# A recorded order table in place of a list scheduler, with four v buffers, six raw buffers and a split of batch 0's exponent inputs, in a fused linear-attention and gated-FFN kernel

## The chip, the cores and the metric

The kernel runs on one core of one Trainium2 chip. The metric is device microseconds of one execution. Five engines work side by side: PE (TensorE, matrix products), DVE (VectorE), ACT (ScalarE), POOL (GpSimd) and SP (SyncE), whose queue issues every DMA here.

## The reference

Linear attention over 8 batches, 8 heads, 576 positions and head dimension 64, then a feed-forward block of width 512 to 1024 and back, with a convolution of three taps and a sigmoid gate:

```
def phi(x):
    proj = np.einsum('bhsd,df->bhsf', x, w_phi)
    proj = proj - np.max(np.abs(proj), axis=-1, keepdims=True)
    return np.concatenate([np.exp(proj), np.exp(-proj)], axis=-1)
q_p, k_p = (phi(q), phi(k))
kv = np.einsum('bhsf,bhsd->bhfd', k_p, v)
z = np.sum(k_p, axis=2)
num = np.einsum('bhsf,bhfd->bhsd', q_p, kv)
den = np.einsum('bhsf,bhf->bhs', q_p, z)[..., None] + 1e-06
attn = num / den
...
h = np.maximum(x @ w_in, 0.0)            # x: attn, heads joined
conv_out = sum(conv_w[k] * hp[:, k:k + S, :] for k in range(3))
out = (h * (1 / (1 + np.exp(-conv_out)))) @ w_out
```

The feed-forward weights come in double precision and are rounded on the chip.

## The kernel before

**Attention.** A unit is one piece of one batch's q or k: `project` loads raw data (tiles rk, rq; tag raw), multiplies it with `w_phi` on PE (tiles pk, pq in PSUM), and takes the maximum of the absolute value along the features on DVE (mk, mq). For every q and for the k of batches 1 to 7, DVE then subtracts that maximum into an SBUF tile (sk, sq), and ACT makes the two exponentials of it (ke; for q after a transpose tp on PE, qe). For the k of batch 0 the subtraction is left out: ACT negates the maximum (the small `mk<-mk` instruction) and makes the exponential straight out of PSUM with the maximum as a bias, one instruction of 128 columns for each of the unit's column groups (`ke<-pk,mk`). The list `KBU` says for each of batch 0's five units and each of its two halves which of the two ways is taken: 'b' is the bias, any other letter the subtraction. A k unit then multiplies ke with v (`kv`, accumulated in PSUM, copied to kvf). A q unit multiplies qe with kvf (`nm`); the denominator dn (on ACT for the batches in `DNA`, else on DVE), its reciprocal rc and the product x follow.

In tile names the numbers after the letters are batch (where it is kept), head group, column piece h, and half: rk0_0_2_1 is batch 0, group 0, piece 2, second load.

**Feed-forward.** The 4608 positions are cut into 11 chunks. For each: xt (transposes of x), xh and xl (a high and a low part), hp (three products for each of 4 x 8 blocks), h, c (convolution), a sigmoid over the whole chunk (ACT has to load its table before it, and the exponential's table again afterwards), gh and gl, op, os and the store. hp and op need no exponentials and are the bulk of PE's work. The weights' rounding (w_r, w_t, win_hi, win_lo, cw) is spread over DVE, ACT and POOL in the first part of the run.

**What sets the order.** Every instruction group is first recorded with `plan.add` (engine, a cost in ns, what it reads and writes, a rank). `Plan.order` is a list scheduler: it keeps a clock for each engine from these costs, and picks at each step the engine that is free first and on it the ready work of the lowest rank. The ranks are shifted by a table of numbers, `NUDGE`. Buffers are given out in the same pass (`Plan.place`). The result is one static order for each engine; each engine then runs its own list and waits only for what its instructions need. SP's list is of this kind too: a DMA that waits for a free buffer holds up all DMAs behind it.

Of the kernel before, what the change touches and what calls it, by code (L numbers as in the profile page):

```python
# [7 lines left out]
F32 = mybir.dt.float32  # L8
# [3 lines left out]
AF = mybir.ActivationFunctionType  # L12
# [4 lines left out]
F = 128  # L17
DM, FF = 512, 1024
P = 128
# [16 lines left out]
LANDING = 1600  # L36
PSUM_G = 4
# [12 lines left out]
SLACK = 60.0  # L50
# [9 lines left out]
RAW = 5  # L60
QS = 2
QE = 3
V = 2
OS = 2
KVF = 6
KBU = ('bb', 'bb', 'bb', 'bb', 'bb')
DNA = (0, 1)
# [3 lines left out]
NUDGE = """  # L71
# [43 lines left out]
"""  # L115
EDGE = [64 * n for n in EDGES]
NCH = len(EDGE) - 1
HW = max(b - a for a, b in zip(EDGE, EDGE[1:]))
TC = max(HW, 450)


class Piece:


    def __init__(self, pool, shape, dtype, name, slots, psum=False):
# [18 lines left out]
class Plan:  # L144
# [90 lines left out]
    def order(self):  # L235
# [6 lines left out]
        if len(shift) == len(self.groups):  # L242
            for w in self.works:
                w.rank += shift[w.group]
# [65 lines left out]
def kernel(  # L310
# [252 lines left out]
    def q_unit(b, qd, h, r):  # L563
        n, ps, m, pr = project(qT, b, qd, h, "q", r)
        x = piece([P, n, 2, D], F32, f"x{b}_{qd}_{h}", "x0" if h == 0 else "x", 2 if h == 0 else NXX)
        for q in range(2):
            if h == 0 or q == qd:
                xs[b, q, h] = x
# [276 lines left out]
```

## Time and profile before

| | |
|---|---|
| median of 3 runs | 708.52 us (708.51, 708.52, 711.76) |
| the profiled execution, its own time | 710.4 us |
| its span, first to last instruction | 708.4 us |
| mean granted PE clock | 0.995 |
| PE busy | 693.5 us, 98% |
| DVE, ACT, POOL busy | 478.5, 430.9, 72.6 us |

The span is the time between the first and the last instruction; what the execution takes beside it is not in the trace. Busy is the time in which at least one instruction of the engine ran. The end of a matmul is modelled, so that a busy PE need not be at its peak. PEclk, where a view shows it, is the clock that PE was granted, as a share of full speed.

### The profile page before, as it was taken

What the parts mean: (1) busy time and instruction counts of PE and PEld (TensorE: products, weight loads), DVE (VectorE), ACT (ScalarE), POOL (GpSimd) and SP (SyncE); (2) the same over time, 40 slices, a digit from 0 to 9 for tenths busy, and PEclk for the clock granted to TensorE, in tenths of its full rate; (3) what the DMA queues carried; (4) which work ended last, traced back from release to release, by engine and by line L of the source; (5) the groups of instructions that cost most, each with busy time, mean ns of one, the idle gap of its engine ahead of it and who ended that gap; (6) DMA issues with size and microseconds to landing.
All of it is one profiled execution on the core that took longest, in us unless ns stands there. A gap on an engine that the chain in (4) does not pass through costs nothing. (4 is left out here: it accounts for less than half of the span.)

```text
span 708.4 us, 22055 instructions
## 1 busy us (share of the span) xinstructions
PE 693.5 (98%) x9484; PEld 639.3 (90%) x9484; DVE 478.5 (68%) x1030; ACT 430.9 (61%) x821; POOL 72.6 (10%) x103
## 2 busy tenths in 40 slices
PE   6998999999999999999999999999999999999998
PEld 5886899899999999999999989999998899999997
DVE  4797998989796286776538675788259544567350
ACT  7977788785774465674349365755567343655351
POOL 0343213350010010000001000100100000101000
PEclk9999999999999999999999999999999999999999
DMA  7563543341212022222202311112002110000001
GB/s 211 163 203 112 153 116 101 103 110 50 69 58 61 22 71 79 73 70 66 64 13 76 106 42 46 57 33 61 27 27 70 35 40 15 14 24 13 36 27 52
DMA packets 46609, 49.00 MB, mean 69 GB/s; under 512 B 6320, under 2 KB 44464, under 8 KB 46512
## 3 DMA queue, kind: packets, MB, share of 16 engines
q1 hardware_dynamic: 46512, 47.59, 22.6%
q8 instruction: 75, 1.23, 0.7%
q14 instruction: 22, 0.18, 0.1%
HBM read 38.13 MB, written 9.44 MB: 67 GB/s over the span
## 5 line engine op out<-in xcount | busy, mean ns | idle before, releaser
L698 DVE SCALAR_TENSOR_TENSOR c<-h,cw,c 128x254 f32<-128x254 f32 (+11 forms) x256 | 122.7, 520 | 100.0 <-ACT c L688 98.7
L675 PE MATMUL hp<-xh,win_hi 128*128 128x448 f32 (+2 forms) x352 | 128.7, 366 | 0.8 <-ACT h L685 0.7
L739 PE MATMUL op<-gh,wout_hi 128*128 128x448 f32 (+3 forms) x352 | 127.6, 362 | 0.0
L739 PE MATMUL op<-gl,wout_hi 128*128 128x448 f32 (+3 forms) x352 | 124.7, 354 | 0.1
L739 PE MATMUL op<-gh,wout_lo 128*128 128x448 f32 (+3 forms) x352 | 124.3, 353 | 0.0
L675 PE MATMUL hp<-xh,win_lo 128*128 128x448 f32 (+2 forms) x352 | 123.9, 352 | 0.0
L675 PE MATMUL hp<-xl,win_hi 128*128 128x448 f32 (+2 forms) x352 | 123.8, 352 | 0.0
L582 ACT ACTIVATE qe<-tp 128x512 f32<-128x512 f32 (+1 forms) x160 | 79.8, 566 | 46.3 <-PE tp L578 46.0
L518 ACT ACTIVATE ke<-sk 128x512 f32<-128x512 f32 (+1 forms) x140 | 74.2, 595 | 41.2 <-DVE sk L492 22.0
L685 ACT ACTIVATE h<-hp 128x448 f32<-128x448 f32 (+2 forms) x88 | 45.5, 518 | 65.0 <-PE hp L675 63.7
L593 PE MATMUL nm<-kvf,qe 128*64 128x65 f32 x2304 | 78.9, 224 | 0.3 <-ACT qe L582 0.2
L682 POOL COPY h<-h 128x3 f32<-128x3 f32 x64 | 28.0, 437 | 478.3 <-DVE c L707 262.5
L593 PEld LDWEIGHTS nm<-kvf,qe 128*64 128x64 f32 x2304 | 73.3, 139 | 3.9 <-issue 2.7
L549 PE MATMUL kv<-v,ke 128*64 128x65 f32 x2048 | 72.5, 226 | 4.5 <-DMA v<-in_vt_dram 3.0
L549 PEld LDWEIGHTS kv<-v,ke 128*64 128x64 f32 x2048 | 66.5, 140 | 8.7 <-ACT w_t L391 3.3
L675 PEld LDWEIGHTS hp<-xh,win_hi 128*128 128x128 f32 x352 | 66.1, 188 | 7.1 <-issue 1.5
L739 PEld LDWEIGHTS op<-gh,wout_hi 128*128 128x128 f32 x352 | 66.2, 188 | 4.7 <-issue 1.2
L739 PEld LDWEIGHTS op<-gl,wout_hi 128*128 128x128 f32 x352 | 66.3, 188 | 4.0 <-DVE gl L719 0.3
L739 PEld LDWEIGHTS op<-gh,wout_lo 128*128 128x128 f32 x352 | 66.4, 189 | 3.3
L675 PEld LDWEIGHTS hp<-xl,win_hi 128*128 128x128 f32 x352 | 66.0, 188 | 3.5
L675 PEld LDWEIGHTS hp<-xh,win_lo 128*128 128x128 f32 x352 | 66.2, 188 | 3.1
L719 DVE TENSOR_TENSOR gl<-c,gh 128x896 fp32r<-128x896 f32 (+3 forms) x44 | 43.5, 1025 | 34.1 <-ACT gh L716 34.0
(58 smaller groups left out, 965.2 us busy)
## 6 DMA issues: line engine op xcount, KB each, us to landing
v<-in_vt_dram SPq DMA_DIRECT2D x80, 130.0 KB, 2.5
rk<-in_kT_dram SPq DMA_DIRECT2D x64, 128.0 KB, 2.6
rq<-in_qT_dram SPq DMA_DIRECT2D x64, 128.0 KB, 2.3
w_r<-in_w_in_dram SPq DMA_DIRECT2D x8, 512.0 KB, 4.1
w_r<-in_w_out_dram SPq DMA_DIRECT2D x8, 512.0 KB, 3.7
out_dram<-os SPq DMA_DIRECT2D x12, 191.0 KB, 2.0
out_dram<-os SPq DMA_DIRECT2D x12, 161.0 KB, 1.8
out_dram<-os SPq DMA_DIRECT2D x8, 225.0 KB, 2.3
```

Source lines behind the costliest of these rows:

```text
L518: act(*((627, 520) if n == 4 else (417, 306)), lambda s=s, e=e, j=j: nc.scalar.activation(out=e[s](), in_=pr[j](), func=AF.Exp, scale=1.0 ...
L549: nc.tensor.matmul(out=kp()[a : a + 64, s, t // 2 * VW : (t // 2 + 1) * VW], lhsT=es[j][s]()[:, t, a : a + 64], rhs=vs[t // 2]()[:, c : c ...
L582: act(*((597, 478) if n == 4 else (384, 264)), lambda s=s, tp=tp, qe=qe: nc.scalar.activation(out=qe()[:, s], in_=tp(), func=AF.Exp, scale ...
L593: nc.tensor.matmul(out=ps_()[a : a + 64, t, :], lhsT=qe()[:, s, t, a : a + 64], rhs=kv[b, q][j]()[:, s, p0 * VW : (p0 + 1) * VW], start=(s ...
L675: nc.tensor.matmul(out=ps()[:, :W], lhsT=w, rhs=x, start=(p == 0 and k == 0), stop=(p == 3 and k == 2))
L682: pool(405, 375, lambda hs=hs, old=old: nc.gpsimd.tensor_copy(out=hs()[:, :3], in_=old[0]()[:, w0 - old[1] : w0 - old[1] + 3]), [(old[0], ...
L685: act(*cols(49, 0.84, W, 121), lambda ps=ps, hs=hs: nc.scalar.activation(out=hs()[:, 3 : 3 + W], in_=ps()[:, :W], func=AF.Relu), w_(ps), [ ...
L698: lambda f=f, hs=hs, j=j, lo=lo, hi=hi: nc.vector.scalar_tensor_tensor(out=c4()[:, f, lo - t0 : hi - t0], in0=hs()[:, at(lo) + j - 1 : at( ...
L719: vec(*cols(67, 1.04, 2 * N, 87), lambda f=f, a=a, gh4=gh4, gl4=gl4: nc.vector.tensor_tensor(out=gl4()[:, a : a + 2, :N], in0=c4()[:, f : ...
L739: nc.tensor.matmul(out=ps()[:, :N], lhsT=w, rhs=x, start=(i == 0), stop=(i == 23))
```

## The change

The list scheduler is no longer asked for the order. A table, `ORDER`, holds 3205 numbers, one for each recorded work, in the order in which they are emitted; `listed` walks it and gives each tile the free buffer that was used longest ago. `V` goes from 2 to 4 (buffers for v), `RAW` from 5 to 6 (raw q and k). `KBU` takes the subtraction for both halves of batch 0's first unit and for the second half of the other four. `DNA` goes from batches 0 and 1 to batches 0 to 3. The switches MP, NB, MG and FD are all 0, so that the code under them is not run; changed costs (LANDING, in `dma`, for c) have no effect either while the table is used.

```
-RAW = 5
+RAW = 6
-V = 2
+V = 4
-KBU = ('bb', 'bb', 'bb', 'bb', 'bb')
-DNA = (0, 1)
+KBU = ('uu', 'bu', 'bu', 'bu', 'bu')
+DNA = (0, 1, 2, 3)
-NUDGE = """
-53 -82 26 0 25 32 6 -88 6 4 51 -2 9 39 73 113 -3 -14 69 181 -79 -37 21 -53 33 40 52 95 -55 44 101 14 13 -125 102 67
...
+ORDER = """
+3 0 178 4 5 6 7 8 9 179 180 195 181 194 182 18 217 183 189 184 185 188 191 186 197 196 23 190 2 286 216 219 19 198
...
+    def listed(self, keys):
+
+        out, last = [], {}
+        for i, key in enumerate(keys):
+            w = self.works[key]
+            for p in w.pieces:
+                if p.slot is None:
+                    free = [s for s in p.slots if s not in self.holder or self.holder[s].left == 0]
+                    p.slot = min(free, key=lambda s: last.get(s, -1))
+                    self.holder[p.slot] = p
+                p.left -= 1
+                last[p.slot] = i
+            assert all(d.end for d in w.after)
+            w.end = 1.0
+            out.append(w)
+        return out
+
     def order(self):
+        keys = [int(x) for x in ORDER.split()]
+        if len(keys) == len(self.works):
+            return self.listed(keys)
```

The number of PE instructions stays at 6024, and PE changes between its three tile shapes (whole array, 64 columns, 64 x 64) 151 times before and 151 times now. On ACT the biased exponentials of 128 columns go from 72 to 32, the plain ones from 140 to 152, the negations of a maximum from 10 to 4, dn from 20 to 40, and the table loads from 18 to 22. On DVE the subtractions sk go from 70 to 76, and dn from 60 to 40.

**SP, the start.** SP's DMAs from the sixth on, before (rk, rq: raw k and q; v; w0_r and so on: raw weights):

```order
L346 DMA rk0_0_2_0_86<-in_kT_dram 128x256
L346 DMA v0_0_0_0_89<-in_vt_dram 128x260
L346 DMA v0_0_0_1_97<-in_vt_dram 128x260
L346 DMA rk0_0_2_1_103<-in_kT_dram 128x256
...
L346 DMA v1_0_0_0_225<-in_vt_dram 128x260
L346 DMA rq0_0_1_1_239<-in_qT_dram 128x256
L346 DMA rk1_0_0_0_260<-in_kT_dram 128x128
L346 DMA v0_0_2_0_299<-in_vt_dram 128x260
L346 DMA v0_0_2_1_303<-in_vt_dram 128x260
```

and the same place now:

```order
L452 DMA w0_r_97<-in_w_in_dram 128x1024
L452 DMA rk0_0_2_1_99<-in_kT_dram 128x256
L452 DMA v0_0_0_0_113<-in_vt_dram 128x260
L452 DMA rq0_0_1_0_138<-in_qT_dram 128x256
L452 DMA rk0_0_2_0_140<-in_kT_dram 128x256
L452 DMA v0_0_1_1_171<-in_vt_dram 128x260
L452 DMA v0_0_1_0_182<-in_vt_dram 128x260
L452 DMA rk0_1_1_0_186<-in_kT_dram 128x256
L452 DMA v0_0_2_0_225<-in_vt_dram 128x260
L452 DMA v0_0_2_1_232<-in_vt_dram 128x260
```

The two loads of v for unit (0, 2), v0_0_2_0 and v0_0_2_1, move from the 24th and 25th place to the 14th and 15th; a weight load of 512 KB now stands ahead of rk0_0_2_1, and the two halves of that unit's raw k have changed places.

**ACT, the start.** ACT's first exponentials of units (0, 0) and (0, 1) before:

```order
L522 ACTIVATE ke0_0_0_1_1_145<-pk0_0_0_1_93,mk0_0_0_1_119 128x128
L522 ACTIVATE ke0_0_0_1_0_179<-pk0_0_0_1_93,mk0_0_0_1_119 128x128 x2
L488 ACTIVATE mk0_0_1_0_136<-mk0_0_1_0_136 128x4
L488 ACTIVATE mk0_0_1_1_147<-mk0_0_1_1_147 128x4
L522 ACTIVATE ke0_0_1_0_0_190<-pk0_0_1_0_105,mk0_0_1_0_136 128x128 x4
L488 ACTIVATE mk0_0_2_0_184<-mk0_0_2_0_184 128x4
L522 ACTIVATE ke0_0_1_1_1_212<-pk0_0_1_1_107,mk0_0_1_1_147 128x128 x4
L522 ACTIVATE ke0_0_1_1_0_237<-pk0_0_1_1_107,mk0_0_1_1_147 128x128 x3
L400 ACTIVATE w0_r_161<-w0_r_161 128x512
```

and now:

```order
L653 ACTIVATE ke0_0_0_1_0_111<-sk0_0_0_1_107 128x256
L506 ACTIVATE w0_r_97<-w0_r_97 128x512
L653 ACTIVATE ke0_0_0_1_1_134<-sk0_0_0_1_107 128x256
L497 ACTIVATE w0_t_152<-w0_t_152,bias_e_136 128x512
L598 ACTIVATE mk0_0_1_0_154<-mk0_0_1_0_154 128x4
L657 ACTIVATE ke0_0_1_0_1_184<-pk0_0_1_0_115,mk0_0_1_0_154 128x128
L657 ACTIVATE ke0_0_1_0_0_190<-pk0_0_1_0_115,mk0_0_1_0_154 128x128 x3
L653 ACTIVATE ke0_0_1_1_1_194<-sk0_0_1_1_158 128x512
L653 ACTIVATE ke0_0_1_1_0_196<-sk0_0_1_1_158 128x512
L657 ACTIVATE ke0_0_1_0_0_190<-pk0_0_1_0_115,mk0_0_1_0_154 128x128
```

Half of a unit's eight biased instructions for one half j have become two wide ones that read sk, which DVE writes; two instructions of the first weight, w0_r and w0_t, stand among them earlier than before.

**PE, where chunk 0's transposes come in.** PE's rows from the last nm of unit (0, 2) of batch 0 to the transposes xt that read its x, before:

```order
L593 MATMUL nm0_0_2_1_1077<-kvf0_0_1_409,qe0_0_2_1_954 64x65 x16
L534 MATMUL kv1_1_0_1103<-v1_0_0_1_487,ke1_0_0_0_1_589 64x130 x2
...
L578 MATMUL tp0_1_2_0_1122<-idn_177,sq0_1_2_0_1038 128x128 x4
L645 MATMUL xt0_0_1135<-idn_177,x0_0_1_682 128x128 x2
L645 MATMUL xt0_0_1135<-idn_177,x0_0_2_1034 128x128
```

and now:

```order
L766 MATMUL nm0_0_2_1_948<-kvf0_0_1_384,qe0_0_2_1_828 64x65 x16
L684 MATMUL kv1_0_1_719<-v1_0_2_0_844,ke1_0_2_1_1_929 64x65 x4
...
L584 MATMUL pk1_1_1_0_1019<-wbd_f_68,rk1_1_1_0_657 64x128
...
L751 MATMUL tp0_1_2_1_1042<-idn_300,sq0_1_2_1_993 128x128 x4
L751 MATMUL tp0_1_2_0_1053<-idn_300,sq0_1_2_0_998 128x128 x4
L818 MATMUL xt0_1_1078<-idn_300,x0_0_1_673 128x128 x2
L818 MATMUL xt0_1_1078<-idn_300,x0_0_2_1047 128x128
```

Between the nm and the first xt that reads x0_0_2 stood 8 rows of kv and 4 of tp (counted as matmuls); now 32 of kv, 16 of pk and 8 of tp stand there.

## Rows read from the trace of the kernel before

**Rows 1.** The page's part 1: busy time, share of the span, instructions.

```profile
PE 693.5 (98%) x9484; PEld 639.3 (90%) x9484; DVE 478.5 (68%) x1030; ACT 430.9 (61%) x821; POOL 72.6 (10%) x103
```

**Rows 2.** Windows: start and end, length, busy by engine, PEclk, DMA share, GB/s.

```profile
0.00:17.70 17.70, 11.66 (x233) 10.10 (x235) 7.32 (x16) 13.43 (x49) 0.44 (x6) 1.00 0.71 211
17.70:75.00 57.30, 52.74 (x1169) 45.86 (x1166) 47.93 (x101) 47.22 (x126) 21.60 (x17) 0.94 0.53 158
75.00:110.00 35.00, 34.99 (x822) 31.89 (x821) 33.77 (x72) 26.48 (x59) 7.69 (x6) 1.00 0.47 135
150.00:690.69 540.69, 540.55 (x6565) 502.49 (x6564) 352.02 (x775) 309.18 (x525) 28.53 (x59) 1.00 0.17 49
```

**Rows 3.** PE's waits over the run: us in total, times, longest.

```profile
PE kv L549 <- DMA v<-in_vt_dram: 3.0, 2, 2.7
PE xt L645 <- DVE x L607: 1.9, 1, 1.9
PE pk L474 <- DMA rk<-in_kT_dram: 1.4, 1, 1.4
PE kv L549 <- ACT ke L518: 1.3, 1, 1.3
PE spare L376 <- POOL bias_e L369: 1.0, 1, 1.0
PE hp L675 <- ACT h L685: 0.7, 1, 0.7
PE pk L474 <- ACT ke L522: 0.6, 1, 0.6
```

**Rows 4.** PE's timeline, 3 to 21 us: start, length, instructions, idle time before.

```profile
3.85 2.63 PE L474 MATMUL pk<-wbd_f,rk 64*64 64x128 f32 x64
7.89 0.67 PE L474 MATMUL pk<-wbd_f,rk 64*64 64x128 f32 x16 [1.40 <-DMA rk<-in_kT_dram]
...
11.35 2.24 PE L549 MATMUL kv<-v,ke 128*64 128x65 f32 x64
16.30 0.45 PE L549 MATMUL kv<-v,ke 128*64 128x65 f32 x8 [2.71 <-DMA v<-in_vt_dram]
```

**Rows 5.** SP's timeline: the load rk0_0_2_1, and both v loads of unit (0, 2).

```profile
4.62 0.33 SPq L346 DMA_DIRECT2D rk<-in_kT_dram  x1
...
13.96 0.86 SPq L346 DMA_DIRECT2D v<-in_vt_dram  x2
```

**Rows 6.** Windows around the two stretches at a lower clock (columns as in group 2).

```profile
18.00:22.50 4.50, 4.24 (x67) 3.76 (x66) 2.95 (x5) 4.50 (x19) 4.15 (x4) 0.62 0.62 189
55.00:60.00 5.00, 5.00 (x100) 4.83 (x100) 4.62 (x9) 4.17 (x11) 2.55 (x2) 0.66 0.35 108
```

**Rows 7.** Windows at the start, for the rate of the DMAs.

```profile
4.50:6.00 1.50, 1.50 (x52) 1.25 (x48) 0.76 (x2) 0.53 (x3) 0.00 (x0) 1.00 0.99 248
...
10.50:12.00 1.50, 1.50 (x53) 1.33 (x49) 0.49 (x1) 1.50 (x7) 0.00 (x0) 1.00 1.02 373
```

**Rows 8.** ACT's timeline: runs of biased and of plain exponentials.

```profile
17.38 2.25 ACT L522 ACTIVATE ke<-pk,mk 128x128 f32<-128x128 f32 x8
...
30.06 1.56 ACT L518 ACTIVATE ke<-sk 128x256 f32<-128x256 f32 x4
...
40.86 1.14 ACT L518 ACTIVATE ke<-sk 128x512 f32<-128x512 f32 x2
```

**Rows 9.** ACT's groups by form: busy us and mean ns of one.

```profile
L391 ACT ACTIVATE w_t<-w_t,bias_e 128x512 int32<-128x512 int32 x16 | 12.0, 762 | 0.6 <-DVE w_t L388 0.6
...
L601 ACT ACTIVATE dn<-nm 128x4 f32<-128x4 f32 x16 | 3.3, 204 | 3.8 <-PE nm L593 3.8
```

**Rows 10.** DVE's groups by form: the subtraction sk, both widths.

```profile
L492 DVE TENSOR_TENSOR sk<-pk,mk 128x512 f32<-128x512 f32 x56 | 36.8, 679 | 0.0
...
L492 DVE TENSOR_TENSOR sk<-pk,mk 128x256 f32<-128x256 f32 x14 | 5.4, 415 | 0.0
```

**Rows 11.** ACT's timeline around one chunk's sigmoid, with a table load on either side.

```profile
310.12 1.28 ACT L704 ACT_TABLE_LOAD   x1
311.42 3.21 ACT L704 ACTIVATE c<-c 128x3600 f32<-128x3600 f32 x1
314.64 1.28 ACT L518 ACT_TABLE_LOAD   x1
```

More of the change, by code (lines that the diff above doesn't have):

```diff
@@ L35 @@
 TABLE = 1283
-LANDING = 1600
-PSUM_G = 4
+LANDING = 1700
 STAY = 0.0
@@ L49 @@
 HQ = 2
-SLACK = 60.0
 M0 = 10.0
@@ L59 @@
 XB = 4
-RAW = 5
+RAW = 6
 QS = 2
 QE = 3
-V = 2
+V = 4
 OS = 2
 KVF = 6
-KBU = ('bb', 'bb', 'bb', 'bb', 'bb')
-DNA = (0, 1)
+KBU = ('uu', 'bu', 'bu', 'bu', 'bu')
+DNA = (0, 1, 2, 3)
 CA = 1
 EDGES = (0, 6, 13, 20, 27, 33, 40, 47, 54, 60, 67, 72)
-NUDGE = """
[43 rows of a table removed]
-"""
+ORDER = """
[130 rows of a table added]
+"""
+PSUM_G = 4
+MP = 0
+NB = 0
+MG = 0
+FD = 0
 EDGE = [64 * n for n in EDGES]
@@ L157, in add @@
         w.before = []
-        w.ready = 0.0
+        w.ready = w.end = 0.0
         w.group = self.groups.setdefault((self.group, eng), len(self.groups))
@@ L240, in order @@
         table, tiled, pipe, port = "Exp", 0, 0.0, {"DVE": 0.0, "POOL": 0.0}
-        shift = [0.25 * int(x) for x in NUDGE.split()]
-        if len(shift) == len(self.groups):
-            for w in self.works:
-                w.rank += shift[w.group]
         out = []
@@ L301, in order @@
             for o in w.before:
-                o.ready = max(o.ready, w.end + HANDOVER[e, o.eng] + (SLACK if o.eng == "PE" and e != "PE" else 0))
+                o.ready = max(o.ready, w.end + HANDOVER[e, o.eng])
                 o.left -= 1
@@ L344, in dma @@
     def dma(outp, inp, kb, rank, reads=(), writes=(), takes=()):
-        cost = {130: 650, 128: 550, 64: 300, 512: 1600}.get(kb, 100 + 2 * kb)
-        plan.add("SP", cost, 450, lambda: nc.sync.dma_start(out=outp(), in_=inp()), reads, writes, rank, takes)
+        cost = ({130: 470, 128: 465, 64: 310, 512: 1550} if FD else {130: 680, 128: 620, 64: 350, 512: 1550}).get(kb, 100 + 2 * kb)
+        plan.add("SP", cost, 240 if FD and kb in (130, 128, 64) and reads == () else 475, lambda: nc.sync.dma_start(out=outp(), in_=inp()), reads, writes, rank, takes)
     def vec(cost, hold, emit, reads, writes, rank, takes=(), port=False):
@@ L463, in project @@
             dma(lambda u=u: raw[u](), lambda q=q, c0=c0: src[b, q, :, c0 : c0 + w], w // 2, r - 3.0, writes=w_(raw[u]))
-        ps = [psum([P, 2 * n * F], f"p{nm}_{i}", M + G if b == 0 and kind == "k" else G) for i in range(2)]
+        ps = [psum([P, 2 * n * F], f"p{nm}_{i}", M + G if b == 0 and kind == "k" else GM if MP else G) for i in range(2)]
         m = [piece([P, 2, 2 * n], F32, f"m{nm}_{i}", "m", 6) for i in range(2)]
@@ L467, in project @@
               for i in range(2)]
+        if MG and h == 0:
+            both = piece([P, 2 * n, 2, F], F32, f"s{nm}", kind + "s", KS if kind == "k" else QS)
+            pr = [None if biased[i] else both for i in range(2)]
         def emit(u):
@@ L479, in project @@
             mm(222 * n, lambda u=u: emit(u), w_(raw[u], wbd_f), [(ps[0], u), (ps[1], u)], r + 0.01 * u,
-               takes=[x for x in (*m, *pr) if x is not None], tiled=2)
+               takes=list(dict.fromkeys(x for x in (*m, *pr) if x is not None)), tiled=2)
         for i, p in enumerate(ps):
@@ L492, in project @@
                     lambda i=i, view=view: nc.vector.tensor_tensor(
-                        out=pr[i](), in0=view(), in1=m[i]()[:, 0].unsqueeze(2).broadcast_to([P, 2 * n, F]),
-                        op=ALU.subtract), w_(p) + [(m[i], 0)], w_(pr[i]), ri - 0.1)
+                        out=pr[i]()[:, :, i] if MG and h == 0 else pr[i](), in0=view(), in1=m[i]()[:, 0].unsqueeze(2).broadcast_to([P, 2 * n, F]),
+                        op=ALU.subtract), w_(p) + [(m[i], 0)], [(pr[i], i if MG and h == 0 else None)], ri - 0.1)
         return 2 * n, ps, m, pr
@@ L509, in k_unit, with __init__, __call__ @@
         es = []
+        if MG and h == 0:
+            ee = [piece([P, 2, 2, F], F32, f"ke{b}_{qd}_{h}_{s}", "ke0", 2) for s in range(2)]
+            plan.group = f"{name}e"
+            for s in (1, 0):
+                if pr[0] is not None and pr[1] is not None:
+                    act(627, 520, lambda s=s: nc.scalar.activation(out=ee[s](), in_=pr[0](), func=AF.Exp, scale=1.0 - 2.0 * s),
+                        w_(pr[0]), w_(ee[s]), r, table="Exp")
+                    continue
+                for j, p in enumerate(ps):
+                    for i in range(2):
+                        act(393, 250, lambda s=s, i=i, j=j, p=p: nc.scalar.activation(
+                            out=ee[s]()[:, i, j], in_=p()[:, i * F : (i + 1) * F], func=AF.Exp, scale=1.0 - 2.0 * s,
+                            bias=m[j]()[:, 1 - s, i : i + 1]), [(p, None), (m[j], 1 - s)], [(ee[s], (i, j))], r + j, table="Exp")
+            class Part:
+                def __init__(self, e, j):
+                    self.e, self.j = e, j
+                def __call__(self):
+                    return self.e()[:, :, self.j]
+            es = [[Part(ee[s], j) for s in range(2)] for j in range(2)]
+            kes = ee
         for j, p in enumerate(ps):
+            if es and h == 0 and MG:
+                break
             rj = r + n // 2 * j
@@ L538, in k_unit @@
                 plan.group = f"{name}m{q}"
-                mm(880, emit, w_(*es[0], *es[1], vs[q]), w_(*kvps[b, q]), r + 1.0 + 4.0 * q, tiled=1)
+                mm(880, emit, w_(*(kes if MG else [*es[0], *es[1]]), vs[q]), w_(*kvps[b, q]), r + 1.0 + 4.0 * q, tiled=1)
             return
@@ L568, in q_unit, with emit_tp, emit @@
                 xs[b, q, h] = x
+        if MG and h == 0:
+            plan.group = f"t{b}_{qd}_{h}_0"
+            tp = psum([P, 4, P], f"tp{b}_0", GM)
+            qe = piece([P, 2, 4, P], F32, f"qe{b}_0", "qe", QE)
+            def emit_tp():
+                for i in range(4):
+                    nc.tensor.transpose(out=tp()[:, i, :], in_=pr[0]()[:, i // 2, i % 2], identity=idn())
+            mm(109 * 4, emit_tp, w_(pr[0], idn), w_(tp), r, takes=(qe,), soft=50)
+            for s in (1, 0):
+                act(597, 478, lambda s=s: nc.scalar.activation(out=qe()[:, s], in_=tp(), func=AF.Exp, scale=1.0 - 2.0 * s),
+                    w_(tp), [(qe, s)], r, table="Exp")
+            ps_ = psum([P, 4, VW], f"nm{b}_0", GM + ["n_0"] * (NB > 0))
+            dn = piece([P, 4], F32, f"dn{b}_0", "dn", 4)
+            rc = piece([P, 4], F32, f"rc{b}_0", "rc", 4)
+            def emit():
+                for i in range(4):
+                    for s in (1, 0):
+                        for a in (0, 64):
+                            nc.tensor.matmul(out=ps_()[a : a + 64, i, :], lhsT=qe()[:, s, i, a : a + 64],
+                                             rhs=kv[b, i // 2][i % 2]()[:, s, a // 64 * VW : (a // 64 + 1) * VW],
+                                             start=(s == 1), stop=(s == 0))
+            plan.group = f"n{b}_{qd}_{h}_0"
+            mm(234 * 4, emit, [(qe, 0), (qe, 1)] + w_(*kv[b, 0], *kv[b, 1]), w_(ps_), r, takes=(dn, rc, x), tiled=1)
+            if b in DNA:
+                act(207, 95, lambda: nc.scalar.activation(out=dn(), in_=ps_()[:, :, D], func=AF.Copy, bias=1e-6), w_(ps_),
+                    w_(dn), r - 0.3)
+            else:
+                vec(150, 66, lambda: nc.vector.tensor_scalar(out=dn(), in0=ps_()[:, :, D], scalar1=1e-6, scalar2=None,
+                                                             op0=ALU.add), w_(ps_), w_(dn), r - 0.3)
+            vec(172, 85, lambda: nc.vector.reciprocal(out=rc(), in_=dn()), w_(dn), w_(rc), r - 0.3)
+            vec(424, 332, lambda: nc.vector.tensor_tensor(
+                out=x().rearrange("p t j d -> p (t j) d"), in0=ps_()[:, :, :D],
+                in1=rc().unsqueeze(2).broadcast_to([P, 4, D]), op=ALU.mult), w_(ps_, rc), [(x, 0), (x, 1)], r - 0.3)
+            return
         for j in range(2):
@@ L583, in q_unit @@
                     out=qe()[:, s], in_=tp(), func=AF.Exp, scale=1.0 - 2.0 * s), w_(tp), [(qe, s)], rj, table="Exp")
-            ps_ = psum([P, n, VW], f"nm{nm}", GM)
+            ps_ = psum([P, n, VW], f"nm{nm}", GM + ["n_0"] * (NB > 0) + ["n_1"] * (NB > 1 and h == 0))
             dn = piece([P, n], F32, f"dn{nm}", "dn", 4)
@@ L687, in h_part @@
             if CA:
-                act(*cols(49, 0.84, N, 121), lambda f=f, hs=hs: nc.scalar.activation(
+                act(*cols(188, 0.83, N, 110), lambda f=f, hs=hs: nc.scalar.activation(
                     out=c4()[:, f, :N], in_=hs()[:, at(t0) : at(t1)], func=AF.Copy, scale=cwv()[:, f, 1:2]),
```

171 rows, old and new, of tables (NUDGE, ORDER) are left out of this document.

## The prediction

> **What bounds the kernel now.** I read the page's first part, then the windows, then PE's own waits, and only then the timelines around the longest of these waits. PE is busy for 693.5 of 708.4 us, and no other engine for more than 68% [rows 1]. So the matrix products set the time, and the change leaves their number alone; it can win only what PE idles, and what PE runs below its full clock. The windows say where that is. From 150 to 690 us PE is busy for 540.55 of 540.69 us, and from 75 to 110 it lacks 0.01 us; up to 75 us it is busy for 11.66 + 52.74 = 64.4 us, so that 10.6 us are idle there, of which 1.0 is the time before its first matmul [rows 2, 3]. The reader should see that 9.6 of the 10.6 are waits in the attention of the first two batches: 3.0 us for v, 1.9 for x (at the transposes of chunk 0), 1.4 for raw k, 1.3 for exponentials ke, 0.6 for a PSUM tile that biased exponentials still read, and about 1.4 in small ones [rows 3]. The clock is the second loss. In two stretches it is granted at a mean of 0.62 over 4.5 us and 0.66 over 5 us, the lower of its two levels being one half (1.2 GHz): that costs 4.5 x 0.38 = 1.7 us and 5 x 0.34 = 1.7 us [rows 6]. The first follows PE's idle 2.71 us up to 16.30 us [rows 4], the second the wait of 1.9 us for x [rows 3]; after the wait of 1.4 us there is none. In all 13.0 us can be had, and no more.
>
> **The base.** The profiled execution took 710.4 us, 2.0 beside its span; the sum is made against it. The median of the runs, 708.52, lies 1.9 us lower, about the price of one stretch at half clock, so that the profiled execution may hold one more than the usual one.
>
> **The change, part by part.**
>
> The start, up to the end of unit (0, 1)'s products with v. Before, these 64 instructions of kv end at 11.35 + 2.24 = 13.6 us [rows 4]. Now ACT decides: it can begin when the first pk (0.67 us from 3.85) and two subtractions and maxima have run, 5.9 us as an estimate. Up to the last exponential of the unit it has four plain ones of 256 (1.56 us), two weight instructions that now stand among them (0.76 each, taken alike), eight biased ones (2.25) and two plain ones of 512 (1.14) [rows 8, 9]: 6.5 us, so 12.4, and half of the kv behind it (1.1) gives 13.5. The same end, but with 16 matmuls of pk1_1 not yet done and 8 of pq done instead: 8 fewer, at 2.63 us for 64 instructions (32 matmuls) some 0.6 us. The raw k here is late in a new way: ahead of rk0_0_2_1 stand 512 KB of weight instead of 128 of k and 260 of v. At 248 GB/s 124 KB more take 0.5 us; at the 373 GB/s that a stretch with weight loads shows, 512 KB take 1.4 us against 1.6 for the 388 [rows 7], so it could also land 0.2 earlier. PE runs dry 8 matmuls sooner. Below: -0.5; above: +1.7. I take **+0.5 us**.
>
> The v loads of unit (0, 2). They were issued at 13.96 us [rows 5], just after the kv that held both buffers had ended, and PE waited 2.71 and 0.3 us for them. Now they are the 14th and 15th DMA and have buffers of their own, so they land long before. What is late next is ke: eight biased (2.25) and two plain exponentials (1.14) after 12.4 are done at 15.8 [rows 8]; PE has pk1_1 and half of pq0_1 to run meanwhile (24 matmuls, 2.0 us, to 15.5), and then the half whose exponentials came first. So nothing is left of the wait: **-3.0**; if ACT is a microsecond and a half later, -1.5.
>
> Exponentials later on. From 18 us on ACT is busy for 4.50 of 4.50 us [rows 6], and batch 0 now asks less of it: 40 biased instructions fewer at 2.25/8 = 0.28 us are 11.2 us, against 8 plain ones at 0.57 and 4 at 0.39, 6.1 us [rows 8]: 5.1 us less. Also the DVE copy frees the PSUM tile after one subtraction instead of eight exponentials. Of the 2.1 us of such waits (ke 1.3, and 0.8 of the small ones) I take two thirds off: **-1.4** (0 to -2.1).
>
> The wait for x. It was 1.93 us behind 12 matmuls. Now 24 matmuls of kv more (48 instructions at 2.24 for 64, 1.7 us), 16 of pk (1.3) and 4 of tp stand in between [rows 4]: over 3.0 us, more than the wait. **-1.9** (0 if DVE comes late with x).
>
> The clock. With both long waits gone the causes of both stretches go. But the start now holds a wait of about 2 us for raw k, nearer to 1.9 (which was followed by one) than to 1.4 (which was not). I take one of two away: **-1.7** (0 to -3.4).
>
> What is added. DVE gets 4 x 0.679 + 2 x 0.415 = 3.5 us of subtractions [rows 10]; 2.2 of it falls before 17.7 us, where DVE is busy for 7.3 of 17.7 us [rows 2], the rest into its 9.4 idle us up to 75. ACT gets 20 dn at 0.20, 4.1 us [rows 9], in batches 2 and 3, and four table loads, 4 x 1.28 = 5.1 us [rows 11], both from some 100 us on, where it idles for 231 of 540 us [rows 2] and PE has hp and op. The only late wait of PE so far was 0.7 us [rows 3]. I take **+0.5** (0 to 4).
>
> Sum: 0.5 - 3.0 - 1.4 - 1.9 - 1.7 + 0.5 = -7.0, so 710.4 - 7.0 = 703.4. From the median with every term it is 701.5; if the 1.9 us between the two was a stretch at half clock, the clock term is nothing there, and the median becomes 703.2. I forecast 702.5, own range 700.8 to 704.9.
>
> **A rule against the change.** One sigmoid in the trace has a load of 1.28 us on either side, and PE does not wait at that place [rows 2, 11]. The Trainium skill, in "ScalarE: Activation LUTs", section "Table sets: the hidden batching unit", says to group activations by table set, since every switch costs a load; by that rule four more loads are 5.1 us more, and if ACT were the bound the sum would be 708.5. The trace agrees on the price of a load (its page has 1283 ns too), not on its weight here.
>
> **The rivals.**
>
> DVE becomes the bound. Up to 75 us it has 9.4 us of idle time after 17.7 [rows 2]; 1.3 of added work and 7.0 us less time leave 1.1. From 75 to 110 it runs at 33.77 of 35. For it: so little slack. Against: ahead of the x that PE waited for, the new order puts three weight instructions of DVE fewer and leaves cw for later. If DVE keeps 5 us of its idle time, PE gains 9.4 - 1.3 - 5 = 3.1: 707.3 against the profiled execution, about 706.5 for the median.
>
> The wait for v turns into one for ke, so that the change does not do what it says. If ACT starts late (the weight instruction in its third place waits for 512 KB), half of the 3.0 stays, and the half clock with it: 703.4 + 1.5 + 1.7 = 706.6, the median about 705.7.
>
> More goes. No wait at the start reaches 1.9 us, both stretches at half clock vanish, and the start term is nothing: 703.4 - 1.7 - 0.5 - 0.5 = 700.7; the median about 699.7.
>
> Slower, the rule above as a mechanism of this kernel. ACT is away for 1.28 + 3.21 + 1.28 = 5.8 us at each of ten sigmoids, with the second load now close behind, while hp and op have two PSUM buffers that only ACT empties. If PE stood still for one load each time, that is 12.8 us: 703.4 + 12.8 = 716.2. It decides from 0.9 us each on. For it: the table has no margin that the trace shows. Against: the pair of loads around 311 us cost PE nothing [rows 2, 11].
>
> **How the numbers follow.** 0.5% of 708.52 is 3.5 us, about what a measurement of this kernel tells from no change: faster is below 705.0, slower above 712.1. Chances: forecast 0.48, more goes 0.17, DVE 0.17, ke for v 0.11, slower 0.07. The range 699.0 to 707.5 leaves out the slow case and the far ends of the others. Faster: 0.48 + 0.17, and 0.05 of the two cases around 706; same 0.23; slower 0.07.
>
> **What would show it.** Right: no wait of kv for v, none of xt for x, PE idle for under 5.5 us between its first matmul and 75 us, one or no stretch at half clock, PE still without a gap after 150 us. Wrong: waits of kv or tp for ke or sk between 10 and 60 us, DVE without idle time from 20 to 110 us while PE waits, or waits of hp and op for ACT around the table loads.

## The result and the profile after

The changed kernel takes 698.25 us (median of four executions, 697.28 to 699.51), beside it the kernel before 709.04: a ratio of 0.984, 95% interval 0.981 to 0.987. It is faster, as forecast, but by 10.8 us where I had 6 to 7, and it lies 0.75 us below the range. The profiled execution took 697.28 us, against 710.4 for the one of before, so the ledger to be closed has 13.1 us (12.9 of span).

Part 1 of the page after (columns as in [rows 1]):

```profile
span 695.5 us, 21959 instructions
## 1 busy us (share of the span) xinstructions
PE 686.6 (99%) x9484; PEld 634.7 (91%) x9484; DVE 478.8 (69%) x1016; ACT 428.7 (62%) x811; POOL 61.4 (9%) x103
```

PE is busy 6.9 us less than before [rows 1], with the same 9484 records of matmuls. That is the first thing to see: a matmul at half clock takes longer, so that 3.4 of the 6.9 us are the clock's [rows 6], but for the other half no step of the prediction allowed. The windows after (columns as in [rows 2]):

```profile
0.00:17.70 17.70, 14.78 (x338) 13.12 (x340) 10.98 (x21) 13.00 (x40) 2.99 (x8) 1.00 0.76 237
17.70:75.00 57.30, 55.22 (x1273) 49.86 (x1270) 55.32 (x119) 48.77 (x119) 18.13 (x15) 1.00 0.60 178
75.00:110.00 35.00, 34.77 (x751) 31.66 (x753) 33.12 (x70) 26.76 (x61) 8.51 (x7) 1.00 0.46 131
150.00:690.00 540.00, 540.00 (x6367) 502.60 (x6366) 341.73 (x733) 306.59 (x527) 22.93 (x62) 1.00 0.16 47
```

Up to 75 us PE idles 75 - 14.78 - 55.22 = 5.0 us, 4.0 without the time before its first matmul; it was 9.6 [rows 2]. The clock is whole in every window; before, two stretches were at a lower one [rows 6]. PE's waits after (us in total, times, longest):

```profile
PE pk L584 <- DMA rk<-in_kT_dram: 2.4, 2, 1.9
PE hp L848 <- ACT qe L755: 1.1, 1, 1.1
PE spare L482 <- POOL bias_e L475: 1.0, 1, 1.0
PE pq L584 <- DVE sk L602: 0.3, 1, 0.3
PE tp L751 <- DVE sq L602: 0.2, 1, 0.2
PE pq L584 <- DMA rq<-in_qT_dram: 0.2, 1, 0.2
```

The waits for v, x and ke of [rows 3] are gone; the wait for raw k is 0.5 us longer, and the one of 1.1 us for qe is new in this list. PE's timeline at the start (start, length, instructions, idle time before):

```profile
3.85 1.77 PE L584 MATMUL pk<-wbd_f,rk 64*64 64x128 f32 x48
7.51 0.67 PE L584 MATMUL pk<-wbd_f,rk 64*64 64x128 f32 x16 [1.89 <-DMA rk<-in_kT_dram]
...
10.40 2.48 PE L684 MATMUL kv<-v,ke 128*64 128x65 f32 x64
12.81 1.10 PE L584 MATMUL pk<-wbd_f,rk 64*64 64x128 f32 x32
13.73 0.62 PE L584 MATMUL pq<-wbd_f,rq 64*64 64x128 f32 x16
14.28 2.09 PE L684 MATMUL kv<-v,ke 128*64 128x65 f32 x64
```

SP's timeline has the two v loads of unit (0, 2), and ACT's the last exponentials that the products of unit (0, 1) read:

```profile
7.12 0.80 SPq L452 DMA_DIRECT2D v<-in_vt_dram  x2
```

```profile
10.75 1.16 ACT L657 ACTIVATE ke<-pk,mk 128x128 f32<-128x128 f32 x4
```

Three things are to be seen. The loads leave at 7.12 us, 6.8 us earlier than before (13.96, [rows 5]). The products of unit (0, 2), which waited 2.71 us up to 16.30 us before [rows 4], now end at 16.4. And two rows of the same 64 matmuls are 2.48 and 2.09 us long, with no idle time listed in either: the first had to wait for exponentials (ACT's last of that unit ends at 11.9 us, in the middle of the row), 0.4 us in all, in stops that the view does not show. Two of them can be read from the starts in the trace: at 11.70 and 11.96 us a matmul starts 0.14 us behind the one before it, just when one of these exponentials has ended.

### The profile page after: what moved, and what is told of

The parts are those of the page before. It is cut to its first block, busy times and chain, and to the rows that moved or that the text cites. A ratio compares the mean times of both kernels' runs of the same rounds, so it can differ in the third digit from the quotient of the medians.

```text
span 695.5 us, 21959 instructions
## 1 busy us (share of the span) xinstructions
PE 686.6 (99%) x9484; PEld 634.7 (91%) x9484; DVE 478.8 (69%) x1016; ACT 428.7 (62%) x811; POOL 61.4 (9%) x103
## 4 chain that ended last, share of the span: by engine, by line
PE 92%; ACT 3%; DVE 2%; DMA 2%; issue 0%; POOL 0%; SPq 0%; ACTq 0%; DVEq 0%
PE op L912 29%; PE hp L848 28%; PE nm L766 9%; PE kv L684 8%; PE pq L584 5%; PE tp L751 4%; PE pk L584 4%; PE xt L818 3%; PE kv L669 2%; ACT ke L657 1%; DMA rk<-in_kT_dram 1%; DMA w_r<-in_w_in_dram 1%; DVE w_t L494 0%; ACT ke L653 0%; DMA rq<-in_qT_dram 0%
## 5 line engine op out<-in xcount | busy, mean ns | idle before, releaser
L871 DVE SCALAR_TENSOR_TENSOR c<-h,cw,c 128x194 f32<-128x194 f32 (+11 forms) x256 | 118.1, 511 | 56.3 <-ACT c L861 55.9
L653 ACT ACTIVATE ke<-sk 128x512 f32<-128x512 f32 (+1 forms) x152 | 85.2, 599 | 30.4 <-DVE sk L602 29.9
L755 ACT ACTIVATE qe<-tp 128x512 f32<-128x512 f32 (+1 forms) x160 | 82.0, 560 | 31.9 <-PE tp L751 31.4
L684 PE MATMUL kv<-v,ke 128*64 128x65 f32 x2048 | 69.0, 222 | 0.0
L684 PEld LDWEIGHTS kv<-v,ke 128*64 128x64 f32 x2048 | 64.3, 138 | 2.4 <-issue 1.4
L595 DVE TENSOR_REDUCE mk<-pk 128x4 f32<-128x512 f32 (+1 forms) x80 | 49.1, 629 | 24.2 <-PE pk L584 24.0
L880 DVE TENSOR_TENSOR c<-c,h 128x448 f32<-128x448 f32 (+3 forms) x88 | 48.6, 593 | 24.8 <-ACT c L877 24.7
```

What stands on the lines that cost most here:

```text
L595: lambda i=i, view=view: nc.vector.tensor_reduce(out=m[i]()[:, 0], in_=view(), axis=AX, op=ALU.max, apply_absolute_value=True), w_(p), [(m ...
L653: act(*((627, 520) if n == 4 else (417, 306)), lambda s=s, e=e, j=j: nc.scalar.activation(out=e[s](), in_=pr[j](), func=AF.Exp, scale=1.0 ...
L684: nc.tensor.matmul(out=kp()[a : a + 64, s, t // 2 * VW : (t // 2 + 1) * VW], lhsT=es[j][s]()[:, t, a : a + 64], rhs=vs[t // 2]()[:, c : c ...
L755: act(*((597, 478) if n == 4 else (384, 264)), lambda s=s, tp=tp, qe=qe: nc.scalar.activation(out=qe()[:, s], in_=tp(), func=AF.Exp, scale ...
L871: lambda f=f, hs=hs, j=j, lo=lo, hi=hi: nc.vector.scalar_tensor_tensor(out=c4()[:, f, lo - t0 : hi - t0], in0=hs()[:, at(lo) + j - 1 : at( ...
L880: vec(*cols(66, 1.04, N, 86), lambda f=f: nc.vector.tensor_tensor(out=c4()[:, f, :N], in0=c4()[:, f, :N], in1=hss[f]()[:, at(t0) : at(t1)] ...
```

## The experiments

A ratio is always to the kernel before, run beside it. Since that kernel's median differs from one group of runs to the next (708.2 to 710.8), a distance "from the changed kernel" is reckoned from 0.984 of the median beside it; the intervals of the two ratios together leave 2 to 3 us either way. In the runs all but the order, all biased, plain exponentials in part of the units, and five raw buffers, the PSUM banks are written down as well (those of the kernel whose order it is, but for a few), which the edits shown leave out.

**The changed kernel again.**

> The changed kernel as it is, beside the others of this call, so that they can be set against it: 698.3, between 697.3 and 699.5.

698.4 us, ratio 0.984 (0.981 to 0.986).

**The buffers alone.** The order of before, its rows and PSUM banks written down, and:

```diff
-RAW = 5
+RAW = 6
-V = 2
+V = 4
```

> The order of the kernel before, row for row and with its PSUM banks, but four buffers for v and six for raw q and k; maxima and denominators as before. Theory of the waits (the gain is the waits of the first two batches and the two half-clock stretches behind them): the wait of kv for v at 16.3 us goes (3.0 us in all) and the first half-clock stretch with it (1.7), the wait for x and its stretch stay: 708.5 - 4.7 = 703.8, and 705.5 if exponentials take the place of half of the wait and the stretch stays. Theory of the order (the buffers are worth nothing until the order uses them, because the loads still stand late in SP's queue): 707.5 to 709.

708.06 us, ratio 0.999 (0.997 to 1.001): nothing. PE still waits for v, and SP's timeline shows why:

```profile
PE kv L695 <- DMA v<-in_vt_dram: 2.7, 1, 2.7
```

```profile
10.82 1.10 SPq L463 DMA_DIRECT2D v<-in_vt_dram  x1
12.03 0.37 SPq L463 DMA_DIRECT2D rq<-in_qT_dram  x1
13.85 0.33 SPq L463 DMA_DIRECT2D rk<-in_kT_dram  x1
14.23 0.90 SPq L463 DMA_DIRECT2D v<-in_vt_dram  x2
```

The two v loads have free buffers and still leave at 14.23 us (13.96 before, [rows 5]), because they stand 24th and 25th in SP's queue behind a raw k that waits for PE. The theory of the order has it.

**All but the order.** The order of before with every other part of the change:

```diff
+KBU = ('uu', 'bu', 'bu', 'bu', 'bu')
+DNA = (0, 1, 2, 3)
+RAW = 6
+V = 4
 ORDER: the rows of the kernel before
```

> The order of the kernel before with all the rest of the change: four buffers for v, six for raw k and q, the six halves of batch 0's maxima subtracted on VectorE (each subtraction stands behind its maximum, each plain exponential where the first of its biased ones stood), all denominators on ACT. Twelve rows around 25 us change places, since a slot is not free earlier. Theory that buffers and engines do the work and the table only writes it down: 698 to 701. Theory of the order (the wait for x, the clock behind it and the short waits are the table's): the v wait and one stretch go, 703.5 to 706; if the old order is upset by the new engines, over 708.5.

710.36 us, ratio 1.002 (1.000 to 1.004): no better than the kernel before, as the theory of the order has it in its second case (the old order upset by the new engines). The products before the load end earlier (at 13.0 us, before at 13.6), the load leaves later (at 15.09 us, before at 13.96), and PE waits longer for it:

```profile
PE kv L694 <- DMA v<-in_vt_dram: 5.0, 1, 5.0
```

```profile
15.09 0.90 SPq L462 DMA_DIRECT2D v<-in_vt_dram  x2
```

**The v loads late again**, in the new order:

```diff
-..."v0" if h == 0 else "v", 2 if h == 0 else V)
+..."v0" if h == 0 else "v", 2 if h == 0 or b == qd == 0 else V)
 ORDER:
-215 21 224 208 204 220 205 225 206
+215 21 208 204 220 205 206
...
-26 27 28 289 187
+26 27 28 224 225 289 187
```

> The changed kernel, but the two v loads of unit (0, 2) of batch 0 use the buffers of unit (0, 1) again and stand in SP's queue behind the second weight, so that they are issued when the products of unit (0, 1) have ended. Theory of the waits: PE waits for v again, 1.5 to 2.5 us around 14 to 16.5 us, and if a long wait is what brings the half clock, a stretch of 3.4 us at 0.5 follows and costs 1.7 more: 698.3 + 2 + 1.7 = 702.0 (701.4 to 702.6). Rival, the clock does not hang on this wait: 700.3, clock 1.00 throughout. Rival, the exponentials make up for it: under 699.2.

703.45 us, ratio 0.993 (0.990 to 0.995), some 6 us from the changed kernel, where I had 3.7, a difference that the intervals do not tell apart.

```profile
PE kv L684 <- DMA v<-in_vt_dram: 2.8, 1, 2.8
PE pk L584 <- DMA rk<-in_kT_dram: 2.6, 3, 1.7
```

The wait is back at 2.8 us, and so is a stretch at half clock behind it (a mean clock of 0.97 from 17.7 to 75 us, where the changed kernel has 1.00); both rivals fall. Its executions show what the clock is worth: the two with a mean granted clock of 1.000 took 701.1 and 701.2 us, the five at 0.993 to 0.996 took 703.4 to 705.5.

**Raw k later at the start:**

```diff
-182 18 217 183 189 184 185 188 191 186 197 196 23 190 2 286 216 219
+182 18 186 286 203 202 217 216 183 189 184 185 188 191 197 196 23 190 2 219
```

> The changed kernel, but the raw k on which PE waited 1.89 us at 5.6 us is issued four loads later (two of v, one of q, one of v more, 518 KB ahead of it). The wait becomes about 3.7 us (518 KB at 300 GB/s). Theory of the waits: everything behind it shifts, and as the wait is longer than the 1.93 us that a half-clock stretch followed in the kernel before, one follows here too: 698.3 + 1.8 + 1.7 = 701.8. Rival, a wait so soon after PE's first work brings no half clock: 700.1, clock 1.00 throughout. Rival, ACT's exponentials set the end of unit (0, 1) and the raw k has slack: under 699.0.

702.22 us, ratio 0.990 (0.987 to 0.994). The wait is 3.6 us long, and a window behind it has half the clock:

```profile
8.70:15.70 7.00, 6.01 (x86) 5.02 (x88) 3.31 (x7) 4.11 (x14) 0.00 (x0) 0.51 0.47 131
```

Seven us at 0.51 cost 3.4, twice what I had. So the half clock does follow a wait at the start, if it is long enough, and raw k has no slack.

**All maxima subtracted by ACT**, in the new order (eight rows change places):

```diff
-KBU = ('uu', 'bu', 'bu', 'bu', 'bu')
+KBU = ('bb', 'bb', 'bb', 'bb', 'bb')
```

> The changed kernel with all maxima of batch 0 subtracted by ACT's bias again, as before; each negation stands where the subtraction stood and the biased exponentials where the plain ones stood; eight rows change places, since their PSUM tiles come free later. ACT then has 5.1 us more in the first 30 us. Theory of the waits: exponentials come late again, in sum by the 1.4 us of my term: 699.7. Rival, the plain exponentials are what lets ACT follow the new order at all: 701.5 or more, with waits of kv or pk for ke of 3 us in sum and a half-clock stretch. Rival, they are worth nothing: 698.0 to 698.8.

709.94 us, ratio 1.001 (0.999 to 1.003): the whole gain is gone, 12 us, where my term had 1.4. The theory of the waits has the kind right and the size wrong by a factor of eight. The rival has it, that the plain exponentials are what lets ACT follow the new order at all: 701.5 or more, with 3 us of waits and a stretch at half clock; all three came, and larger.

```profile
PE pk L595 <- ACT ke L668: 5.1, 2, 2.9
PE pk L595 <- DMA rk<-in_kT_dram: 2.1, 1, 2.1
PE pq L595 <- ACT ke L668: 1.3, 1, 1.3
```

pk and pq wait for exponentials that still read the PSUM tile which they are to write (L668 is the biased form). Before, such waits were 0.6 us [rows 3]. The mean granted clock is 0.993, so that 5 us more go to half clock.

**Where the plain exponentials count.** First only those of units (0, 0) and (0, 1), then only those of the three later units:

```diff
+KBU = ('uu', 'bu', 'bb', 'bb', 'bb')
```

> The changed kernel with plain exponentials only in units (0, 0) and (0, 1) (three halves); the halves of (0, 2), (1, 1) and (1, 2) go back to biased ones. Theory that biased exponentials hold PSUM tiles which the new order wants early: most of the 11.5 us come back, since the longest waits of the run with all biased (2.85 us at 16.3 and 2.25 us at 30 us) were those of pk for ke of these later units: 704 to 708, with two half-clock stretches. Rival, the start decides: 699 to 700.5.

```diff
+KBU = ('bb', 'bb', 'bu', 'bu', 'bu')
```

> The changed kernel with plain exponentials only in units (0, 2), (1, 1) and (1, 2); the three halves of (0, 0) and (0, 1) are biased. Theory of the tiles: the waits at 16.3 and 30 us stay away; ACT is later by 0.7 + 1.1 us at the start, of which PE waits for 1.3 at 12 us: 699.5 to 701.5. Rival, the start decides: 705 to 709. If the two runs' losses add up to 11.5 us the parts are independent; if both are small, one of the two is enough.

706.32 us (ratio 0.997, 0.995 to 0.998) and 701.80 (0.992, 0.989 to 0.994): some 9 and 5 us from the changed kernel; their sum of 14 and the 12 of all biased lie too near for the intervals to tell whether the parts overlap. With the first units alone PE waits for tiles of the later ones, as the theory of the tiles has it (PE idles for 3.4 us from 15.1 us on and for 2.25 from 29.7 on); with the later alone one such wait of 2.9 us stays, from 11.0 us on:

```profile
PE pk L595 <- ACT ke L668: 5.6, 2, 3.4
PE pk L595 <- DMA rk<-in_kT_dram: 2.9, 1, 2.9
```

```profile
PE pq L595 <- ACT ke L668: 2.9, 1, 2.9
```

Not all of the 9 us is the tiles': in that profile raw k at the start is waited for 2.9 us (1.9 in the changed kernel's) with a stretch at half clock from 8.1 us on, although the loads stand in the same order. Of the same wait the other profiles of the new order with these loads at their places have between 1.5 and 2.7 us.

**Five raw buffers:**

```diff
-RAW = 6
+RAW = 5
```

> The changed kernel with five raw buffers instead of six; loads of raw q and k then wait for an older tile, and some 400 rows of the table change places with rows of other engines, five of them on their own engine. Theory that the order needs the buffers that it was made with: raw k and q land late from 20 us on, 700 to 704. Rival, five are enough, as six alone gave the kernel before nothing: 698 to 699.

754.99 us, ratio 1.067 (1.064 to 1.071), 58 us from the changed kernel and ten times the most that I had. Each engine runs its own list, so that beside the buffer only the rows count that change places on their own engine; these are six (four of PE, two of SP). That they are not the cause was not tried, but the waits are those for raw loads, all along the run:

```profile
PE pq L594 <- DMA rq<-in_qT_dram: 18.8, 12, 2.2
PE pk L594 <- DMA rk<-in_kT_dram: 16.9, 9, 2.7
PE kv L694 <- DMA v<-in_vt_dram: 6.8, 3, 2.7
```

**No table:** the list scheduler places the works by its ranks.

```diff
-ORDER = """3 0 178 4 5 6 ..."""
+ORDER = """"""
```

> The changed kernel with an empty table: its list scheduler places the same instructions with the same buffers by its ranks, without the corrections that the kernel before had. Theory of the order (buffers and engines are worth nothing unless the order uses them): slower than the kernel before, 712 to 725, with PE's busy time at full clock at 689 us or more, as in the three orders of the list scheduler measured so far, against 686 in the table's. Rival, the buffers make most orders good: under 705.

719.16 us, ratio 1.013 (1.011 to 1.016). PE idles little (12.1 us in the whole run, 11.6 before), but is busy for 700.6 us. Counted in the traces, PE changes 202 times between its three tile shapes; in the kernels before and after it is 151 times. The steps over a change take 43.6 us here and 32.1 before: 0.23 us more for each of the 51.

**Denominators back on VectorE:**

```diff
-DNA = (0, 1, 2, 3)
+DNA = (0, 1)
```

> The changed kernel with the denominators of batches 2 and 3 on VectorE again, at the same places of the table (20 instructions, 4.1 us of ACT, about 3 us of DVE). Theory that PE's order and the first 75 us alone count: no change, within 0.4 us of the changed kernel. Rival, DVE is close to the bound (33.1 of 35 us busy from 75 to 110 us): 1 to 3 us slower. Rival, ACT's 20 instructions more were a cost (my term of 0.5 us): 0.5 faster.

698.78 us, ratio 0.984 (0.981 to 0.986): no difference, as the first theory has it. The rivals are not all told apart from it: half a us to 1 us is less than these runs can show.

**Four attempts at a faster version.** The exchange of two loads; with it two later moves (the rows between those shown are left out); and the first weight's load seven places later, with five instructions on it, without and with those moves:

```diff
-195 181 194 182 18 217 183
+195 181 194 182 217 18 183
```

> The changed kernel with two loads exchanged at the start: the raw k on which PE waited 1.89 us goes ahead of the first weight (512 KB). Theory that the load alone holds the start: the wait falls to 0.5 us or less and the time by 1.4 us, 696.9; and the spread of the times shrinks, since 1.89 us was just short of the 1.93 that a half-clock stretch followed. Rival, ACT's exponentials set the end of unit (0, 1) at 12.9 us anyway: the idle time moves behind the pk and the time stays, 698.0 to 698.6. Rival, the weight, now later, holds up ACT and DVE, whose instructions on it stand among the exponentials: 699 or more.

```diff
 as above, and
-100 499 535 534
+535 534 100 499
...
 58 (the load of weight 1) behind 346 and 347 (raw k)
```

> The changed kernel with three moves of the table: the exchange of the loads at the start as in the run before; the load of weight 1 behind the two raw k of batch 1 that stand next (PE waited 0.52 us for them at 28.35 us, since SP's queue was held by the weight); and one weight instruction of ACT, which waited 1.54 us for VectorE at 71 us, and a denominator behind the two qe on which PE waited 1.14 us at 73.28. Theory that each listed wait is worth its length: 698.3 - 1.4 - 0.5 - 1.1 = 695.3. Rival, each only uncovers the next wait: 697 to 698.

```diff
-195 181 194 182 18 217 183
+195 181 194 217 186 216 286 203 202 18 182 183
...
 19 behind 220; 23, 20 behind 221; 21 behind 223
```

> The changed kernel with the first weight (512 KB) seven places later in SP's queue, behind the raw k, q and v of the first units, and the five instructions of ACT and VectorE on it that stood among the first exponentials behind those of unit (0, 1). Theory that the bytes ahead in the queue hold the start, and the exchange of two loads only chose which of them PE waits for: no wait over 0.7 us before 13 us, no half-clock stretch, the products of unit (0, 1) end 1 us earlier, 697.2, with a smaller spread. Rival, the time won at the start is given back at the next short waits, as in the run with three moves: 698.0 to 699.2.

> The run before with the two later moves too (the load of weight 1 behind two raw k; ACT's weight instruction behind two qe). Theory that what each wait costs adds up: 697.2 - 0.5 - 1.1 = 695.6. Rival, each uncovers the next: 697 to 698.8.

They took 699.06, 698.52, 699.17 and 697.81 us, ratios 0.984, 0.983, 0.985 and 0.983, each with an interval of 0.002 to 0.003 to either side: none differs from the changed kernel. In the first the wait only changes its name, from raw k to the v load behind it. In the third the products of unit (0, 1) end 1.0 us earlier than in the changed kernel, as forecast (11.9 us against 12.9), but those of unit (0, 2) at 16.3, where the changed kernel has 16.4:

```profile
9.44 2.45 PE L684 MATMUL kv<-v,ke 128*64 128x65 f32 x64
...
14.18 2.11 PE L684 MATMUL kv<-v,ke 128*64 128x65 f32 x64
```

In the last the 1.1 us for qe are gone, a stop of pk at the place of the second move is still there under another name, and waits for q and sk stand beside it. The waits of the first, then of the last:

```profile
PE kv L669 <- DMA v<-in_vt_dram: 1.5, 1, 1.5
PE xt L818 <- DVE x L780: 1.0, 1, 1.0
```

```profile
PE pq L584 <- DMA rq<-in_qT_dram: 1.7, 3, 0.7
PE nm L766 <- DVE sk L602: 0.7, 1, 0.7
PE pk L584 <- issue: 0.5, 1, 0.5
```

That each uncovers the next wait fits all four; that each listed wait is worth its length does not hold in any of them. In the first, the rival that the later weight holds up ACT and DVE (699 or more) fits its 699.06 us as well and is not told apart.

## Why the prediction was right, and where it failed

**The start, +0.5.** The listed wait for raw k did grow by this much, from 1.40 to 1.89 us, with the weight load ahead of it. But the term was worked out from ACT: the same end of unit (0, 1), at 13.5 us, with 0.6 us less of other matmuls done. The end came at 12.9 us, so that by this working the term is about nothing; that the 0.5 is met by the wait is luck.

**v, -3.0, and x, -1.9.** Both rows are gone, and undoing the first (v late) brings back 2.8 us and its half clock. But I gave the buffers half the credit. The buffers alone do not make the load earlier; with the 14th place in the queue it leaves at 7.12 us. That this place needs the buffers is argued from their use, not tried alone. The wait for x was not tried by itself: in the old order with all the rest of the change it is 0.3 us, so that the matmuls that the new order puts in between are not shown to be what removes it.

**Exponentials, -1.4.** As a difference between the two profiles the size is near: PE's waits for ke, 1.3 and 0.6 us [rows 3] and 0.8 in smaller ones, are gone, and 1.1 us for qe and 0.5 for subtractions have come. As a price of that part it is wrong, since without it the new order loses 12 us. The term was read from an order that was made for biased exponentials, and such rows do not tell what a part is worth in another order. The raw buffer, which had no term, gave nothing in the old order and cost 58 us when it was taken from the new one.

**The clock, -1.7.** In the two profiles the loss falls from 3.4 us [rows 6] to nothing: the wait at the start came out as long as I feared, and no stretch followed it. Over all executions of the kernel before in these runs (60 that came with a clock), span times one minus mean clock is 2.7 us on average, over nine of the changed one 1.0: a gain of 1.7. So the profiled execution of before held more half clock than the usual one, as the prediction supposed in its paragraph on the base.

**Added work, +0.5.** No wait of hp or op for a table load is in the list, and PE is busy for 540.00 of 540.00 us from 150 us on. A busy PE can hide stops, as is shown below, but the steps from one whole-array matmul to the next add up to 450.8 us, 451.4 before, so that none were added there. The denominators' return to VectorE changes nothing that the runs can show. The rule of the Trainium skill in "ScalarE: Activation LUTs" (section "Table sets: the hidden batching unit") still decides nothing here; how much the four loads would cost in a stretch where ACT is the bound, no run shows. The slower rival and the one on VectorE fall: from 17.7 to 75 us VectorE is now busy for 55.32 of 57.30 us, and in the whole run PE waits 0.5 us for it.

**The step that failed** is the ledger's ceiling: "it can win only what PE idles, and what PE runs below its full clock ... In all 13.0 us can be had, and no more". The profiles' 12.9 us of span are 5.6 of idle time up to 75 us, 0.5 later, 3.4 of clock, and some 3.4 of busy time at full clock, which no term had. Against the sum of -7.0 that is 0.8 more of idle time, 1.7 more of clock and these 3.4; without the 3.4 the time would be 701.7 us, inside the range. Every sign that the prediction named for being right came (no wait for v or x, 4.0 us of idle time where under 5.5 was asked, no stretch at half clock, no gap after 150 us), and none of them looks at how long PE is busy. The table has all profiles. "Idle" is PE's idle time up to its last matmul, "half" what was lost at half clock: half of the time that PE was busy at 1.2 GHz, by the traces.

```
order          kernel                          idle   busy  half  at full clock
of before      before                          11.6  693.5   3.4  690.0
of before      buffers alone                   11.2  692.3   1.7  690.6
of before      all but the order               13.2  691.6   1.7  689.9
no table       no table                        12.1  700.6   1.7  698.9
of the table   changed                          5.5  686.6   0.0  686.6
of the table   changed, again                   5.3  687.2   0.0  687.2
of the table   v late                          10.1  688.2   1.7  686.5
of the table   raw k later                      9.0  689.4   3.0  686.4
of the table   all biased                      13.3  690.6   4.7  685.9
of the table   plain in the first units        12.2  690.3   4.8  685.5
of the table   plain in the later units         8.6  688.6   1.7  686.9
of the table   denominators back                7.1  688.8   1.7  687.1
of the table   two loads exchanged              7.3  687.1   0.0  687.1
of the table   exchange and moves               6.3  688.7   1.7  687.0
of the table   weight late                      6.2  687.8   0.0  687.8
of the table   weight late, moves               5.0  688.2   0.0  688.2
of the table   five raw buffers                48.8  701.7  11.6  690.0
```

In the main it goes with the order: 689.9 to 690.6 us in the order of before, 685.5 to 688.2 in that of the table. But the run with five raw buffers, whose engines keep their lists but for six rows, has 690.0, so the order alone does not settle it. In the other runs of the table's order it is lowest in the two in which PE idles longest (685.9 with all maxima on ACT, 685.5 with plain exponentials in the first units) and highest in the one in which it idles least (688.2 in the last attempt). That attempt idles 0.5 us less than the changed kernel and is busy for 1.6 us more: less idle time is not less time.

What the 3.4 us consist of is shown in part. Where each matmul's start is set against the next one's, and listed idle time and half clock are taken off, the steps add up to 689.7 us before and 686.3 after. Of the difference 2.3 lie inside runs of the small attention products (kv, nm, pk, pq), where the same matmuls follow each other more closely, the rest in runs of whole-array matmuls and in changes of shape, whose number is the same. Short stops as in the row of 2.48 us against 2.09 are busy time in the profile, since a matmul's modelled end lies well behind the next one's start: in the run with all biased two matmuls of kv make a row of 0.28 us, 64 one of 2.09. In these runs of small products 72 steps before and 39 after end just when a semaphore is released; above the mean step they hold 1.0 and 0.1 us. That is 0.9 of the 2.3 us between these two profiles. But in the run with all but the order they hold 0.1 us as well, with 689.9 us at full clock, so such stops do not account for the difference between the orders, and the cause of the 3.4 us stays open.

The Trainium skill says in "Perfetto Trace Analysis", section "Identifying the Most-Contended Engine", that a matrix engine's busy share is no measure of how near it is to its bound, because matmuls are pipelined. The trace agrees: 98% busy before, and 6.9 us less of it after with the same matmuls. One of the two figures that it gives instead, the busy share of weight loads (PEld), is 90% before, 91% after and 89% without a table; it ranks the three kernels as their times do, a point apart each.

## What to carry to other kernels

Busy time of a pipelined engine is no floor: add up its steps from start to start before writing that only idle time can be won, and count changes of tile shape. A price of one part, read from the waits of the old order, holds for that order alone; here the buffers, and buffers and engines together, gave nothing without the order (ratios 0.999 and 1.002). The order without them was not run; with the order in place, undoing one of them lost nothing that shows (denominators), some 6 us (v late), all of the gain (exponentials) or far more (a raw buffer). And a load that comes late has two causes to look up, its buffer and its place in the queue.

## What the runs showed of the hardware

The length of PE's wait alone does not settle whether the half clock follows it. In the 17 profiled executions none of the 16 waits of 1.36 to 1.89 us had a stretch at 1.2 GHz at its end or behind it, all 11 of 2.67 us and more had one, and of the 17 from 1.93 to 2.66 us ten. One stretch, in the run without a table, came with no wait over 0.9 us before it but the one ahead of PE's first matmul. The changed kernel's 1.89 us stands next to this, and its executions differ accordingly: mean clocks of 0.995 to 1.000 go with 700.8 to 697.3 us.
